# Second tile of q and k: loaded in fp32 by the hardware DMA queues and cast on chip

## The chip, the cores and the metric

The kernel runs on one core of one Trainium2 chip. The metric is device time in microseconds for one execution, the median over several runs of the same program. A profiled execution is shown beside it, with its own span.

## The reference

Attention with a sliding window of 128 tokens and four "sink" tokens that every token sees, then a layer norm and a two-layer MLP with a residual. Batch 4, 8 heads, 768 tokens, head size 64, so the MLP works on rows of 512 with an inner size of 2048. All inputs and the output are fp32.

```python
scores = (1/sqrt(D)) * q @ k.T
keep   = (pos_k < n_sink) | ((0 <= pos_q - pos_k) & (pos_q - pos_k < window))
a      = softmax(where(keep, scores, -1e9))
x      = (a @ v) with the heads side by side            # (B, S, 512)
xn     = (x - mean(x)) / sqrt(var(x) + 1e-6) * g_ln
out    = x + relu(xn @ w_ch1) @ w_ch2
```

## The kernel before

**Tiling.** The 3072 tokens are 24 tiles of 128 (`t`), two to a chunk (`c`, twelve chunks, three to a batch element). Per chunk: load q and k, bring them into the transposed layout `kq` (head size on the partitions), multiply for the scores (`sc`), exponentiate on ScalarE (`ex`), mask on VectorE (`mk`), multiply with v (`av`), divide by the row sum (`rc`, `x`), take mean and variance (`bn`, `ag`), center (`xc`), transpose (`trx`, copied out by `evx`), and then the MLP: `ph` is the first layer, in eight blocks per chunk, `rl` its relu on ScalarE, `pc` or `p1` to `p7` the second layer. The first two chunks are handled tile by tile, the rest by chunk.

**Order.** Every step is an operation of a planner (`Plan`) with a priority, the engines that may run it and a cost. `Plan.run` simulates all queues and gives each engine a fixed order; the program is then written out in that order. So a changed cost or a changed set of operations can change the order on any engine. Waits between engines come from semaphores. PE is also given filler matmuls on a `junk` tile where the plan has it idle in the first 24 us.

**Queues.** Three DMA queues matter. SP and ACT issue plain copies (the hardware queues). GpSimd (POOL) issues the copies that cast from fp32 to bf16 (the casting queue); nearly all inputs come that way. The program has eight completion semaphores for the hardware queues together and eight for the casting queue; a ninth transfer of a kind waits at its issue until the first has landed.

**The first chunk.** This is what the change touches. Tile 0 of q and k comes in fp32 by SP and ACT, four transfers of 128 KB (`kld00*`, `qld00*`, line 620) into the buffer `n4a`. It is cast to bf16 on chip in two halves (`cast0` on ScalarE, `cast1` on VectorE, line 637), transposed on PE (`tr000`, `tr001`, line 649) and copied from PSUM into `kq` in four pieces (`ev00**`, line 595, 128x256 each). Tile 1 comes by the casting queue, already bf16, into two `nat` buffers (`kld01`, `qld01`, line 626). It needs no cast: PE transposes it (`tr010`, `tr011`, line 645) and VectorE copies it out in two pieces of 128x512 (`ev010`, `ev011`).

**The order of the first loads on POOL**: `kld01`, `qld01`, `vld0` (v of tile 0), `kld1`, `qld1` (k and q of chunk 1, 256 KB each as bf16, into `n4b`, line 602), `vld1`, `w1ld0`, `w1ld1` (the first two quarters of the first MLP weight, 512 KB each, line 547), `vld2`, `w1ld2`, `vld3`, `w1ld3`, `kld2`, `qld2` (chunk 2, into `n4c`), and so on.

**The order on PE around it**: `tr000 tr001 sc0_0 tr010 tr011 sc1_0 gtt av0 pm11 sc1_1 tr10 tr11 trx0 av1 vp0 sc2_0 sk1 sc2_1 sc3_0 ph0_0 trx1 sc3_1 ph0_1 sv2 av2 ph0_2 sv3 ph0_3 ph0_4 trx2 av3 ph0_5 ph1_0 ph0_6 trx3 ph0_7 ph1_1 tr20 tr21 ...`; **on ScalarE**: `cast0 ev0000 ev0010 ex0_0 ex1_0 ex1_1 ev11 ex2_0 sx1 ex2_1 ex3_0 ex3_1 rl0_0 rl0_1 ...`; **on VectorE**: `cast1 ev0001 ev0011 kts0 ev010 ev011 gt rc0 x0 bn0 ag0 xc0 ev10 evx0 rc1 x1 bn1 ag1 xc1 mk2_0 evx1 mk2_1 vs0 mk3_0 mk3_1 rc2 ...`. Here `tr10`, `tr11` transpose chunk 1, `gtt` and `gt` bring in the layer norm's weight (a load of 2 KB on SP, line 526), `vp0` and `vs0` prepare the sink values, `sk` and `sx` are the sink scores and their exponential, `sv` the sink values' product, `kts0` packs the sink keys.

Of the kernel before, what the change touches and what calls it, by code (L numbers as in the profile page):

```python
# [236 lines left out]
NEG = -1e30  # L237
NEVER = -1e9

PAR = dict(split=(3, 4, 5, 6, 7), gsum=-8.0, guard=183.0, strict=40.0, win=0.4, tr=-8.0, sc=-5.3, sc1=-2.0, av=2.0, trx=9.0, by_dma=4, x_by_dma=2, g_on_w=2, av2=20.0, avi=1.0, behind=5, gtt=9.0, ramp=0.3, vs0=2.6, vpb=12.0,  # L240
           w1p=(0.15, 1.7, 2.05, 2.8), pm=2, w2p=(4.5, 4.51, 4.52, 4.53), by_tile=2, wino=2, vp=(0.0, 0.1, 2.0, 2.1, 4.2, 4.3), ld1=0.05,
           h=dict(av=1.62, avi=0.4, sc=-7.53, sc1=-3.14, tr=-20.67, trx=9.0, xo=-11.34), mkp=(0,), mko=-3.48, vsp=1, soon=0, lb=0, xlag=2.1, llag=2.4, mix=(1.0, 0.5), tzp=16.19, kp=-0.9, half=4, wsum=58.0, flip=1, te=("POOL",), tlead=33.28, rd=0, cpr=20.34, sp=(10.74, 5.73), sq=(-5.24, -23.14, 6.14, 23.93), pos=(0.11, 1.67, 2.3, 8.33, 1.63, 2.3, 3.91), pos4=(7.29, 3.8, 1.67, 7.72))

# [130 lines left out]
def kernel(  # L374
# [218 lines left out]
    def evict(name, prio, n, src, dst, reads, writes, fp=False):  # L593
        du = {"ACT": act(n), "DVE": dve(n) if fp else dve(n, 0.52)}
        P.op(name, du, prio, lambda e: (nc.scalar.copy if e == "ACT" else V.tensor_copy)(dst(), src()),  # L595
             reads=reads, writes=writes)

    def load4(c, nm, prio, loaded):
        b, R = c // RC, c % RC
        p0 = 64 * "kq".index(nm)  # L600
        ap = (k if nm == "k" else q)[b, :, 256 * R:256 * R + 256, :].rearrange("h (p i) d -> p h (i d)", i=4)
        P.op(f"{nm}ld{c}", {"POOL": (0.72, 0.75)}, prio, lambda e: G.dma_start(
            n4_b[c].t[p0:p0 + 64].rearrange("p h i d -> p h (i d)"), ap), writes=[loaded, n4_b[c]], dma=SW_4)

    def chunk(c):
# [3 lines left out]
        T = Buf(f"kq{c}", "kq")  # L609
        kq_b[c] = T  # L610
        if c == 0:
            f0, c0 = n4_b[0], Buf("c0", "hq")
            raw = lambda: f0.t.rearrange("p h i d -> p (h i d)").bitcast(FP32).rearrange("p (h i d) -> p h i d", h=4, i=4)
            cut = lambda: c0.t.rearrange("p a b -> p (a b)")[:, 0:1024].rearrange("p (i h d) -> p i h d", i=4, h=4)
            for x, src in enumerate((k, q)):
                for hh in range(2):
                    ap = src[b, 4 * hh:4 * hh + 4, 0:128, :].rearrange("h (p i) d -> p h (i d)", i=4)
                    p0 = 64 * x + 32 * hh
                    P.op(f"{'kq'[x]}ld00{hh}", {("SP", "ACT")[x]: (0.53, 0.53)}, -110 + hh, lambda e, p0=p0, ap=ap:
                         (nc.sync if e == "SP" else nc.scalar).dma_start(  # L620
                             raw()[p0:p0 + 32].rearrange("p h i d -> p h (i d)"), ap), writes=[f0], dma=HW_F)
            nat = []
            for x, (nm, src) in enumerate((("k", k), ("q", q))):
                nat.append(Buf(f"{nm}n01", "nat"))
                ap = src[b, :, 128:256, :].rearrange("h p d -> p h d")
                P.op(f"{nm}ld01", {"POOL": (0.87, 0.9)}, -50 + 0.1 * x, lambda e, nat=nat[x], ap=ap: G.dma_start(nat.t, ap),  # L626
                     writes=[nat[x]], dma=(SW[0] + PAR["ramp"] * (1 - x), *SW[1:]))
            for t in range(2):
                for hh in range(2):
                    hs = slice(4 * hh, 4 * hh + 4)  # L630
                    pt, half = Buf(f"pt0{t}{hh}", "one"), Buf(f"c0{hh}")
                    done = Buf(f"T0{t}{hh}") if t or not hh else tile_of[0, 0]
                    tile_of[t, hh] = done
                    if t == 0:
                        two = slice(2 * hh, 2 * hh + 2)
                        P.op(f"cast{hh}", {"DVE": dve(512), "ACT": act(512)}, early(0) + 0.01 * hh, lambda e, two=two:
                             (nc.scalar.copy if e == "ACT" else V.tensor_copy)(cut()[:, :, two], raw()[:, two].rearrange("p h i d -> p i h d")),
                             reads=[f0], writes=[c0, half])

                    def tr(e, pt=pt, t=t, hh=hh):  # L640
                        pb = pt.t.bitcast(BF16)[:, 0:512]
                        if t:
                            for h in range(2):
                                for x in range(2):
                                    nc.tensor.transpose(pb.rearrange("p (h k c) -> p h k c", h=2, k=2)[:, h, x],
                                                        nat[x].t[:, 4 * hh + 2 * h:4 * hh + 2 * h + 2, :], ident)
                        else:
                            for i in range(4):
                                nc.tensor.transpose(pb[:, 128 * i:128 * i + 128], cut()[:, i, 2 * hh:2 * hh + 2], ident)
                    P.op(f"tr0{t}{hh}", pe(0.3), early(t) + 0.02 + 0.1 * hh, tr, reads=[*(nat if t else [half]), Bc["ident"]],  # L650
                         hold=[T] + ([] if t else [c0]), writes=[pt])
                    if t:
                        evict(f"ev0{t}{hh}", early(t) + 0.05 + 0.1 * hh, 512,
                              lambda pt=pt: pt.t.bitcast(BF16)[:, 0:512].rearrange("p (m c) -> p m c", m=4),
                              lambda hs=hs: T.t[:, hs.start // 2:hs.start // 2 + 2, :, 128:256].rearrange("p h k c -> p (h k) c"), [pt], [T, done])
                    for a in () if t else range(2):
                        evict(f"ev00{hh}{a}", early(0) + 0.05 + 0.1 * hh + 0.01 * a, 256,
                              lambda pt=pt, a=a: pt.t.bitcast(BF16)[:, 0:512].rearrange("p (i k a g) -> p a k g i", i=4, k=2, a=2)[:, a],
                              lambda a=a, hh=hh: T.t[:, 2 * a + hh, :, 0:128].rearrange("p k (g i) -> p k g i", i=4), [pt], [T, done], fp=True)
        elif c < PAR["by_dma"]:  # L660
            loaded = Buf(f"l{c}")
            for i in range(2):
# [250 lines left out]
    def weight_sums():  # L913
        a = [w1[m][:, 2 * i:2 * i + 2, :] for m in range(2) for i in range(2)]
        get = {n: (lambda i=i: a[i]) for i, n in enumerate(("a11", "a12", "a21", "a22"))}
        held = [Buf(f"ws{i}", "hq") for i in range(2)]
        for i, (x0, x1, op) in enumerate((("a21", "a22", ALU.add), (0, "a11", ALU.subtract),
                                          ("a11", "a21", ALU.subtract), ("a12", 1, ALU.subtract))):
            done = Buf(f"wsum{i}")
            ap = lambda i=i: held[i // 2].t[:, 2 * (i % 2):2 * (i % 2) + 2, :]  # L920
            val = lambda x: ap(x) if isinstance(x, int) else get[x]()
            P.op(f"wsum{i}", {"DVE": dve(1024, 0.52)}, PAR["wsum"] + 3.0 * i, lambda e, ap=ap, x0=x0, x1=x1, op=op, val=val:
                 V.tensor_tensor(ap(), val(x0), val(x1), op=op), reads=Bw1g[0:2] + [wsum[x][1] for x in (x0, x1) if isinstance(x, int)],
                 hold=[held[i // 2]], writes=[done], nb=PAR["wsum"] + 3.0 * i)
            wsum.append((ap, done, held[i // 2]))

# [145 lines left out]
                     reads=[ot, oo], dma=HW_S)  # L1072

    def wino(c, T, hq, h1, quick):
        A = [lambda g=g: hq[g].t.rearrange("p (v k) (s t) -> p k v s t", k=2, s=2) for g in range(2)]
        part = {"a11": lambda g: A[g]()[:, 0, :, :, 0:128], "a21": lambda g: A[g]()[:, 0, :, :, 128:256],
                "a12": lambda g: A[g]()[:, 1, :, :, 0:128], "a22": lambda g: A[g]()[:, 1, :, :, 128:256]}
        if quick:
            h1 = [None] * 4 + h1
        deps = {n: [quick[int(n[1]) - 1] if quick and g == 0 else h1[4 * g + (0 if n[2] == "1" else 1)::2][:2] for g in range(2)] for n in part}  # L1080
        sb = {}

        def get(n, g):
# [80 lines left out]
    for c in range(NC):  # L1164
# [5 lines left out]
            attend_tile(2 * c + 1)  # L1170
        else:
            attend(c)
    idle = [[o for z in n4_b if z.ring == f"n4{x}" for o in z.users] for x in "bca"] + [[]]
    for qt in range(4):
        b11, b12, b21, b22 = (w2[qt][:, 2 * i:2 * i + 2, 256 * j:256 * j + 256] for i in range(2) for j in range(2))
        t1, t2, t3, t4 = (w2t[i][:, qt] for i in range(4))
        for i, (o, x0, x1) in enumerate(((t1, b12, b11), (t2, b22, t1), (t3, b22, b12), (t4, b21, t2))):
            P.op(f"w2t{i}_{qt}", {"DVE": dve(512, 0.52)}, 16.0 * PAR["wino"] - 6.0 + qt + 0.1 * i, lambda e, o=o, x0=x0, x1=x1: V.tensor_tensor(
                o, x0, x1, op=ALU.subtract), reads=[Bw2[qt]] + ([Bw2t[i - 1][qt]] if i in (1,) else [Bw2t[1][qt]] if i == 3 else []),
                writes=[Bw2t[i][qt]], after=idle[i])  # L1180

# [98 lines left out]
```

## Time and profile before

| | |
|---|---|
| median of 3 runs | 208.51 us (208.4 to 208.91) |
| profiled execution, its own time | 208.16 us |
| its span | 206.6 us, TensorE at the full granted clock (1.0) |
| PE busy | 199.4 us, 97% of the span |
| DVE, ACT, POOL busy | 179.6, 119.7, 118.7 us |
| casting queue | 13.37 MB written as bf16, 81.7% of the 16 DMA engines' span |
| hardware queue of SP | 13.43 MB, 34.1% |

The profiled execution took 208.16 us, of which its span is 206.6. The remaining 1.6 us lie around the program. A row of the timeline gives the start, the duration, the engine, the line, the operation and how many instructions it merges, and in brackets how long the engine sat idle before it and what ended that. GB/s counts the bytes written; a casting transfer reads twice what it writes.

### The profile page before, as it was taken

To read this page: it belongs to the slowest core of one execution; us is meant where nothing else is said; L and a number is where in the kernel's file an instruction comes from. 1 tells how busy PE (TensorE), PEld (TensorE's weight loads), DVE (VectorE), ACT (ScalarE), POOL (GpSimd) and SP (SyncE) were. 2 spreads that over 40 slices of the span, in tenths; PEclk is the share of its full clock that TensorE was granted. 3 is DMA by queue.
4 is the path that set the end of the run, shared out by engine and by line. 5 is a ranking of instruction groups with operands and counts; after the bars stand their busy time and mean duration, and the time that the engine had idled before them with its cause. 6 is when DMAs were issued, how large, how long until landed. Compare 5 with 4: busy or idle time off the path is not lost.

```text
span 206.6 us, 6790 instructions
## 1 busy us (share of the span) xinstructions
PE 199.4 (97%) x2766; PEld 165.6 (80%) x2766; DVE 179.6 (87%) x437; ACT 119.7 (58%) x187; POOL 118.7 (57%) x170
## 2 busy tenths in 40 slices
PE   6888999999999999999999999999999999999994
PEld 2557996674698897898998988988988988988993
DVE  7589769899599899899989989989989989998693
ACT  3649477839555655666486486485486585560620
POOL 7977475279039029959649949968627229125000
PEclk9999999999999999999999999999999999999999
DMA  5999999999999999999999999899976411210302
GB/s 117 146 195 195 197 181 205 199 158 171 186 200 124 124 191 101 121 174 101 175 152 137 113 159 143 109 171 114 194 117 101 128 33 23 106 32 19 108 27 84
DMA packets 101341, 27.55 MB, mean 133 GB/s; under 512 B 89652, under 2 KB 99128, under 8 KB 101304
## 3 DMA queue, kind: packets, MB, share of 16 engines
q0 software_dynamic: 67712, 13.37, 81.7%
q1 hardware_dynamic: 33304, 13.43, 34.1%
q8 instruction: 22, 0.36, 0.7%
q10 hardware_dynamic: 288, 0.26, 0.4%
q14 instruction: 15, 0.12, 0.2%
HBM read 27.31 MB, written 6.29 MB: 163 GB/s over the span
## 4 chain that ended last, share of the span: by engine, by line
PE 90%; DMA 3%; DVE 3%; POOL 2%; issue 0%; DVEq 0%
PE one L1109 31%; PE one L1027 20%; PE one L958 12%; PE one L1058 7%; PE one L1020 7%; PE pair L854 5%; PE pair L802 4%; DMA n4b<-in_q_dram 3%; PE one L672 1%; PE pair L721 1%; POOL nat L626 1%; PE one L714 1%; DVE xnt L907 1%; DVE kq L595 1%; POOL vn L589 0%; DVE st L874 0%
## 5 line engine op out<-in xcount | busy, mean ns | idle before, releaser
L1027 PE MATMUL one<-xnt,w 128*128 128x256 bf16 x384 | 46.8, 273 | 0.0
L814 ACT ACTIVATE pe<-pair 128x1024 bf16<-128x1024 f32 (+1 forms) x40 | 36.3, 963 | 18.2 <-PE pair L802 18.2
L1037 ACT ACTIVATE hq<-one 128x512 bf16<-128x512 f32 x58 | 33.4, 590 | 17.9 <-PE one L1020 9.4
L1027 PEld LDWEIGHTS <-w 128*128 128x128 bf16 x384 | 36.3, 98 | 4.0
L1109 PEld LDWEIGHTS <-hs 128*128 128x128 bf16 x320 | 31.0, 98 | 4.0
L882 POOL TENSOR_SCALAR st<-st 128x1 f32<-128x1 f32 x24 | 6.4, 266 | 44.4 <-DVE rec L868 27.5
L826 DVE TENSOR_TENSOR pe<-pe,mask 128x1024 bf16<-128x1024 bf16 (+1 forms) x35 | 27.1, 799 | 1.6 <-ACT pe L814 1.4
L969 ACT COPY tz<-one 128x512 f32<-128x512 f32 x24 | 13.9, 585 | 20.6 <-PE one L958 19.2
L1109 PEld LDWEIGHTS <-hq 128*128 128x128 bf16 x240 | 22.2, 98 | 4.1 <-issue 0.5
L589 POOL DMA_DIRECT2D vn<-in_v_dram x24 | 21.9, 922 | 2.2 <-DMA w<-in_moe_w_ch_dram 1.2
L983 ACT ACTIVATE hq<-hq 128x512 bf16<-128x512 bf16 x24 | 15.1, 630 | 13.1 <-DVE hq L980 12.6
L1109 PE MATMUL one<-w,hq 128*128 128x256 bf16 x160 | 19.2, 273 | 0.0
L980 DVE TENSOR_TENSOR hq<-one,tz 128x512 bf16<-128x512 f32 x24 | 16.4, 684 | 1.9 <-PE one L958 1.0
L1130 DVE TENSOR_TENSOR ot<-one,tm 128x256 f32<-128x256 f32 x40 | 15.9, 412 | 2.1 <-PE one L1109 1.8
L1123 DVE TENSOR_TENSOR tm<-one,x 128x256 f32<-128x256 f32 x40 | 16.6, 414 | 1.2 <-PE one L1109 1.1
L870 DVE TENSOR_TENSOR x<-pair,rec 128x512 bf16<-128x512 f32 x24 | 16.6, 691 | 0.8
L874 DVE BATCH_NORM_STATS2 st<-x 128x6 f32<-128x512 bf16 x24 | 16.5, 687 | 0.2
L1020 PE MATMUL one<-xnt,w 128*128 128x128 bf16 x256 | 16.0, 219 | 0.5 <-DVE xnt L907 0.5
L687 POOL DMA_DIRECT2D nat<-in_q_dram x16 | 14.2, 893 | 3.7 <-DMA w<-in_moe_w_ch_dram 3.7
L938 POOL TENSOR_TENSOR xt<-xnt 128x256 bf16<-128x256 bf16 x16 | 12.2, 778 | 7.1 <-DMA xnt<-xc 7.0
L687 POOL DMA_DIRECT2D nat<-in_k_dram x16 | 14.8, 928 | 2.4 <-DMA w<-in_moe_w_ch_dram 2.4
L1020 PEld LDWEIGHTS <-w 128*128 128x128 bf16 x256 | 14.6, 98 | 1.6 <-issue 0.8
(130 smaller groups left out, 387.7 us busy)
## 6 DMA issues: line engine op xcount, KB each, us to landing
out_dram<-ot SPq DMA_DIRECT2D x17, 256.0 KB
w<-in_moe_w_ch_dram POOLq DMA_DIRECT2D x8, 512.0 KB, 12.8
vn<-in_v_dram POOLq DMA_DIRECT2D x24, 128.0 KB, 6.9
nat<-in_k_dram POOLq DMA_DIRECT2D x17, 128.0 KB, 4.6
nat<-in_q_dram POOLq DMA_DIRECT2D x17, 128.0 KB, 4.9
out_dram<-ot SPq DMA_DIRECT2D x14, 128.0 KB
kq<-nat SPq DMA_TRANSPOSE x32
xnt<-xc SPq DMA_TRANSPOSE x20
```

What stands on the lines that cost most here:

```text
L589: loads[b * RB + r, "v"] = P.op(f"vld{t}", {"POOL": (0.87, 0.9)}, prio, lambda e: G.dma_start(bv.t[:, :, 0:64], v[b, :, 128 * r:128 * (r + ...
L687: lambda e, nat=nat, ap=ap: G.dma_start(nat.t, ap), writes=[nat], dma=SW if c < 6 else (*SW[:2], PAR["llag"]), after=behind(c, 0 if soon e ...
L814: P.op(f"ex{c}{hp}", {"ACT": act(2 * n)}, d + 0.1 + 0.05 * j, lambda e, pp=pp, pb=pb: nc.scalar.activation(pb.t[:, :, 0:n], pp.t[:, :, 0:n ...
L826: V.tensor_mul(pb.t[:, :, 0:n], pb.t[:, :, 0:n], mm),
L870: P.op(f"x{t}", {"DVE": dve(512)}, d + xo + 0.11, lambda e: V.tensor_tensor(x.t.rearrange("p (a h c) -> p a h c", a=2, c=64), pv()[:, :, : ...
L874: P.op(f"bn{t}", {"DVE": fix(0.60)}, d + xo + 0.12, lambda e: V.bn_stats(st.t[:, 8:14], x.t), reads=[x], writes=[st, mv])
L958: nc.tensor.matmul(b.t[:, 128 * h:128 * h + 128], lhsT=lt[:, kk, 128 * h:128 * h + 128], rhs=rh[:, kk, :], start=first and h == 0 and kk = ...
L1020: nc.tensor.matmul(ph.t[:, 128 * s:128 * s + 128], lhsT=w1[u // 2][:, j, 128 * s:128 * s + 128], rhs=xnt.t[:, j, 128 * (u % 2):128 * (u % ...
L1027: nc.tensor.matmul(ph.t[:, 256 * s:256 * s + 256], lhsT=w1[ht // 4][:, j, 128 * (ht % 4):128 * (ht % 4 + 1)], rhs=xnt.t[:, j, :], start=j ...
L1037: nc.scalar.activation(hg.t[:, u % 4, :], ph.t, AF.Relu)
L1109: nc.tensor.matmul(at(r), lhsT=get(left, g)[:, v, s, :], rhs=rhs, start=first and n == 0, stop=n == 7, skip_group_check=True)
L1123: return P.op(f"tm{name}_{c}", {"DVE": dve(256, 1.14)}, pr - PAR["kp"], lambda e: V.tensor_tensor(tm[name].t, at(r), xs[i].t[:, sl], op=AL ...
```

## The change

Tile 1 of q and k is handled as tile 0 is. Four more transfers of 128 KB are issued on SP and ACT right behind those of tile 0, into the buffer `n4c` (which later takes chunk 2, and is free until then). Two casts (`cast10`, `cast11`), two groups of four transposes and four 128x256 copies (`ev01**`) take the place of the two casting loads, eight transposes and two 128x512 copies. The planner's cost of such a hardware load is 0.42 instead of 0.5. Other edits in the diff only name constants (`w2tp`, `we`, `c1p`) at the values that were there, or rewrite `wino` for a case that doesn't occur.

```diff
-HW_F = (0.5, 0.9, 0.9)
+HW_F = (0.42, 0.9, 0.9)
...
         if c == 0:
-            f0, c0 = n4_b[0], Buf("c0", "hq")
+            for t in range(2):
+                f0, c0 = (n4_b[0], Buf("r0b", "n4c"))[t], Buf(f"c0{t}", "hq")
+                n4x.append(f0)
...
+                for x, src in enumerate((k, q)):
+                    for hh in range(2):
+                        ap = src[b, 4 * hh:4 * hh + 4, 128 * t:128 * t + 128, :].rearrange("h (p i) d -> p h (i d)", i=4)
+                        p0 = 64 * x + 32 * hh
+                        P.op(f"{'kq'[x]}ld0{t}{hh}", {("SP", "ACT")[x]: (0.53, 0.53)}, -110 + 2 * t + hh, ...
+                             (nc.sync if e == "SP" else nc.scalar).dma_start(
+                                 raw()[p0:p0 + 32].rearrange("p h i d -> p h (i d)"), ap), writes=[f0], dma=HW_F)
...
-            for x, (nm, src) in enumerate((("k", k), ("q", q))):
-                nat.append(Buf(f"{nm}n01", "nat"))
-                ap = src[b, :, 128:256, :].rearrange("h p d -> p h d")
-                P.op(f"{nm}ld01", {"POOL": (0.87, 0.9)}, -50 + 0.1 * x, lambda e, nat=nat[x], ap=ap: G.dma_start(nat.t, ap),
-                     writes=[nat[x]], dma=(SW[0] + PAR["ramp"] * (1 - x), *SW[1:]))
...
+                    P.op(f"cast{t}{hh}", {"DVE": dve(512), "ACT": act(512)}, early(t) + 0.01 * hh + (PAR["c1p"] if t else 0.0), ...
+                         (nc.scalar.copy if e == "ACT" else V.tensor_copy)(cut()[:, :, two], raw()[:, two].rearrange("p h i d -> p i h d")),
+                         reads=[f0], writes=[c0, half])
...
-                    if t:
-                        evict(f"ev0{t}{hh}", early(t) + 0.05 + 0.1 * hh, 512,
...
+                    for a in range(2):
+                        evict(f"ev0{t}{hh}{a}", early(t) + 0.05 + 0.1 * hh + 0.01 * a, 256,
```

The planner's new orders, up to where they meet the old ones again. **POOL**: `kld1 vld0 qld1 vld1 w1ld0 w1ld1 vld2 w1ld2 vld3 w1ld3 kld2 qld2 ...` and from there as before. **PE**: `tr000 tr001 sc0_0 tr010 gtt av0 tr011 sc1_0 tr10 pm11 sc1_1 trx0 tr11 sc2_0 vp0 av1 ph0_0 sc2_1 sk1 sc3_0 trx1 sc3_1 ph0_2 ph0_1 sv2 av2 sv3 ph0_3 av3 ph0_4 trx2 ph0_5 ph0_6 ph0_7 trx3 ph1_0 tr20 tr21 ph1_1 ...`; from the end of chunk 1's MLP on (`ph2_0`) the order on PE is that of before. **ScalarE**: four issues, `tab`, then `cast00 cast01 ev0000 ev0010 ex0_0 cast11 ev0100 ev0101 ev0110 ev0111 ex1_0 ev10 ex1_1 ex2_0 rl0_0 ex2_1 sx1 ex3_0 ex3_1 rl0_2 rl0_1 ...`. **VectorE**: `ev0001 ev0011 kts0 cast10 gt rc0 x0 bn0 ag0 xc0 evx0 ev11 rc1 x1 bn1 ag1 xc1 mk2_0 evx1 mk2_1 vs0 mk3_0 mk3_1 rc2 ...`.

More of the change, by code (lines that the diff above doesn't have):

```diff
@@ L656, in chunk @@
-                    for a in () if t else range(2):
-                        evict(f"ev00{hh}{a}", early(0) + 0.05 + 0.1 * hh + 0.01 * a, 256,
+                    two = slice(2 * hh, 2 * hh + 2)
+                    P.op(f"cast{t}{hh}", {"DVE": dve(512), "ACT": act(512)}, early(t) + 0.01 * hh + (PAR["c1p"] if t else 0.0), lambda e, two=two, raw=raw, cut=cut:
+                         (nc.scalar.copy if e == "ACT" else V.tensor_copy)(cut()[:, :, two], raw()[:, two].rearrange("p h i d -> p i h d")),
+                         reads=[f0], writes=[c0, half])
```

63 lines of the change are left out of this document (22 added, 41 removed).

## The prediction

> **What bounds the kernel now.** I read the page first.
>
> ```profile
> span 206.6 us, 6790 instructions
> PE   6888999999999999999999999999999999999994
> ```
>
> After the first four slices (20 us) PE has no slack left. From the end of chunk 1 on PE's order is the same in both kernels, so what the change is worth is how much earlier, or later, PE reaches the work that fills it: a shift of the start. The profiled execution took 208.16 us, 0.35 less than the median of 208.51; the sum is made against 208.16 and carried over to the median. About 0.3% (0.63 us) is what a measurement of this kernel can tell from no change.
>
> Second, the chain that ended last, at its beginning.
>
> ```profile
> 1.99 1.08 POOL nat L626
> 3.07 0.90 POOL nat L626
> 3.98 0.88 POOL vn L589
> ...
> 5.50 7.09 DMA n4b<-in_q_dram
> 12.73 0.65 PE one L672 x16
> 13.41 1.23 DVE kq L595
> ...
> 18.75 1.05 PE one L1020 x16
> 20.61 0.89 PE one L1020 x16
> ```
>
> The start hangs on the casting queue: two `nat` issues that the change removes, `vld0`, then `qld1`, whose landing at 12.59 lets PE transpose chunk 1. Last, the timeline of the same stretch.
>
> ```profile
> 1.02 0.90 ACTq L620 DMA_DIRECT2D n4a<-in_q_dram  x2
> ...
> 1.95 1.28 ACT L481 ACT_TABLE_LOAD   x1 [1.95 <-PEq L1261]
> ...
> 5.04 0.62 ACT L637 CAST hq<-n4a 128x512 bf16<-128x512 f32 x1 [1.59 <-DMA n4a<-in_q_dram]
> ...
> 6.43 0.65 ACT L595 COPY kq<-one 128x256 bf16<-128x256 bf16 x2 [0.78 <-PE one L649]
> ...
> 7.05 1.55 POOL L547 DMA_DIRECT2D w<-in_moe_w_ch_dram  x2
> ...
> 7.63 0.41 DVE L695 COPY kts<-kq 64x16 bf16<-64x16 bf16 x2
> ...
> 7.82 0.62 PE L645 MATMUL one<-ident,nat 128*128 128x128 bf16 x8
> 7.92 1.02 ACT L758 ACTIVATE pe<-pair 128x1024 bf16<-128x1024 f32 x1 [0.84 <-PE pair L754]
> ...
> 9.16 1.02 ACT L758 ACTIVATE pe<-pair 128x1024 bf16<-128x1024 f32 x1 [0.22 <-PE pair L754]
> ...
> 10.19 0.42 PE L854 MATMUL pair<-vn,pe 128*128 128x65 bf16 x8 [0.91 <-ACT pe L758]
> ...
> 13.85 1.01 ACT L595 COPY kq<-one 128x1024 bf16<-128x1024 bf16 x1 [0.66 <-PE one L672]
> ...
> 13.98 0.65 PE L854 MATMUL pair<-vn,pe 128*128 128x65 bf16 x16
> ...
> 15.15 0.20 DVE L868 RECIPROCAL rec<-pair 128x8 f32<-128x8 f32 x1
> ...
> 16.15 0.27 ACT L769 ACTIVATE ps<-one 128x128 bf16<-128x128 f32 x1
> ...
> 16.56 2.85 ACT L758 ACTIVATE pe<-pair 128x1024 bf16<-128x1024 f32 x3
> ...
> 19.29 1.15 ACT L1037 ACTIVATE hq<-one 128x512 bf16<-128x512 f32 x2
> ...
> 19.55 1.28 DVE L761 TENSOR_TENSOR pe<-pe,mask 128x1024 bf16<-128x1024 bf16 x2
> ...
> 19.74 0.28 PE L721 MATMUL pair<-vs,ps 32*128 32x260 bf16 x2
> ...
> 24.16 2.84 PE L1020 MATMUL one<-xnt,w 128*128 128x128 bf16 x48
> ```
>
> Two things are to be seen. Tile 1's first exponential (`ex1_0`, 9.16) runs before `av0` (10.19). And `av0` is put down to ScalarE, but its exponential had ended at 8.94: what came at 10.19 was v of tile 0, as the landing below shows. `av0` waits for `vld0`.
>
> **The DMA side.** The next rows are stretches of one microsecond (last column GB/s written) and single transfers (last column: us from issue to landing).
>
> ```profile
> 2.00:3.00 1.00, 1.00 (x3) 0.30 (x2) 1.00 (x9) 1.00 (x1) 1.00 (x1) 1.00 0.67 179
> 3.00:4.00 1.00, 1.00 (x4) 0.35 (x3) 0.87 (x6) 0.44 (x2) 1.00 (x3) 1.00 1.02 335
> 4.00:5.00 1.00, 1.00 (x5) 0.45 (x4) 0.96 (x6) 0.00 (x0) 1.00 (x2) 1.00 0.90 67
> 6.00:7.00 1.00, 1.00 (x15) 0.66 (x11) 0.16 (x1) 0.56 (x2) 1.00 (x2) 1.00 1.98 129
> 9.00:10.00 1.00, 0.28 (x6) 0.23 (x2) 0.17 (x2) 0.83 (x1) 1.00 (x2) 1.00 1.37 174
> ```
>
> ```profile
> vn<-in_v_dram POOLq DMA_DIRECT2D x1, 128.0 KB, 6.2
> n4b<-in_q_dram POOLq DMA_DIRECT2D x1, 256.0 KB, 7.1
> w<-in_moe_w_ch_dram POOLq DMA_DIRECT2D x1, 512.0 KB, 8.8
> w<-in_moe_w_ch_dram POOLq DMA_DIRECT2D x1, 512.0 KB, 10.8
> ```
>
> Tile 0's four transfers are 524 kB and are what moved from 2 to 4 us (179 + 335 kB); ScalarE could cast at 5.04, about 1.0 after the last bytes. Then follows a gap: 67 kB in the microsecond from 4 to 5, half of what the casting queue moves once it runs (129).
>
> *Removed*: 2 x 131 kB from the casting queue, at 129 kB a us 2.0 us; and 1.08 + 0.90 us of issue on POOL. *Added*: 524 kB on the hardware queues, at 335 kB a us 1.6 us, of which about 0.5 fall into the gap. So all that stands behind on the casting queue comes 2.0 - 1.6 + 0.5 = 0.9 us earlier, by this estimate: `qld1` at 11.7 instead of 12.59, `w1ld0` at about 15.0 (before: issued at 7.05, 8.8 to landing, 15.85), `w1ld1` at 17.7 (before: issued at 7.8, landed at 18.6). The ends: 0, if the two kinds of transfer hinder each other by as much as is saved, and 2.0, if the added ones cost the casting queue nothing.
>
> [...]
>
> *`vld0` itself* is less sure. It is issued about 1.0 earlier (second in the queue instead of third; 256 KB of `kld1` ahead of it in place of the two `nat`), which by its 6.2 us gives 9.1. But the 1.6 us of hardware traffic now stand in its way, less 0.5 of gap and 2.0 - 1.5 for `kld1` at 174 instead of `nat` at 129: 0.6 later, 10.8. I take 9.8, between the two: by 10.19 the queue had moved far more than `vld0` and what stood ahead of it, so bytes alone don't set its landing.
>
> *Covered at no cost*: the two more issues on ACT (0.45 each) push the table load to 2.9, done by 4.4 with its first use, before 5.04; if the cover went, tile 0's cast would wait, and that would still be 1.2 us short of `av0`. On SP eight hardware loads use all eight semaphores, so the load of the layer norm's weight and the `vc` loads wait for tile 0's landing at 5.0 rather than being issued from 1.93 on; `gtt` needs the weight at 9.06 and the `vc` loads are first needed in chunk 3. The second fp32 set lands between 6.6 (alone) and 8.1 (sharing half the engines): 4.0 + 1.6 or 3.1, + 1.0. VectorE takes `cast10` after `kts0`, at 8.04, ScalarE `cast11` after `ex0_0`, at 8.94. Both casts of tile 0 are now on ScalarE (0.62 each, to 6.28 instead of 5.79 on two engines), but its copies out of PSUM alternate between the engines as before, and tile 0 stays at 7.6. Were it later, `ex0_0` and `cast11` follow one to one.
>
> **The chain of tile 1.** On PE the order is now `tr010 gtt av0 tr011 sc1_0`: the second half of tile 1 is queued behind `av0`, which waits for `vld0`. Behind them stand `sc1_0` and everything of chunk 1. With `vld0` at 9.8, `av0` ends at 10.25, `tr011` (four of the eight transposes in 0.62) at 10.55. ScalarE has all four 128x256 copies (0.33 each): `ev0110` ends at about 11.0, the other half of `sc1_0` waits for it, and `ex1_0` starts at 11.35, 2.2 us later than the 9.16 of before. If `vld0` came at once, `cast11` would set it: 9.55 + 1.1 = 10.7.
>
> From there ScalarE is the chain: `ex1_0` to 12.4, `ev10` (1.01) 13.4, `ex1_1` 14.4, `ex2_0` 15.4. `av1` runs from 14.45 to 15.1 (before: 13.98). `ph0_0` follows at 15.15, since `w1ld0` is there; `rl0_0` (0.6) ends at 16.75, `ex2_1` at 17.8, `sx1` and two exponentials of 0.95 at 20.0; before, the last of these ended at 19.41. VectorE's row from `rc1` to `evx1` is the same list as before: there it began at 15.15 and let PE go at 18.75; now it begins at 15.2. Then `mk2_1`, `vs0` and the two masks, which ended at 20.83, 2.1 us behind `evx1`, end near 20.9, or 1.28 after the exponentials, 21.2 at the latest.
>
> So tile 1 is about half a us later. What pays for it is the order on PE: `ph0_0` and, from 18.3, `ph0_2` run where PE stood idle, with weights that came 0.9 earlier. Counted on: `ph0_2` to 19.2, `ph0_1` 20.1 (0.89 each), `sv2`, `av2`, `sv3` 21.2 (0.28 and 0.65 a piece), `ph0_3` 22.1, `av3` 22.75, `ph0_4` 23.65, `trx2` about 23.9. Before, PE had the same set behind it at 24.16, where the group of 48 matmuls begins. The sum is 24.16 - 23.9 = 0.25 us gained: 207.9 on the profile's scale, 208.3 as a median. Each us by which `vld0` lands otherwise moves the result by as much, in both directions, break-even being a landing at about 10.05; earlier than 9.1 gains nothing more, as `cast11` and `w1ld0` then set the pace.
>
> **The rivals.**
>
> *The queue is relieved in full.* `vld0` lands by 9.2 and the weights come 1.5 to 2 us earlier: `ex1_0` at 10.7, and the set is done 0.65 earlier still, a gain of 0.9: 207.6. For it: `nat` was the slowest traffic in the rows (129 against 174), and the issue is a us earlier. Against: the hardware traffic stands in exactly this stretch.
>
> *`vld0` is held up by the hardware traffic.* It lands at 10.8 or 11.0 instead of 10.19, and, unlike before, half of tile 1's transposes wait behind `av0`: `ex1_0` at 12.4, ScalarE's row ends past 21, the set at 24.9 to 25.1: 0.75 to 0.95 slower, 209.3 to 209.5. It decides as soon as `vld0` lands after 10.7. For it: PE's new order and the bytes ahead. Against: the issue is earlier. [...]
>
> *The change buys nothing of what it says.* The second fp32 set lands after 9, so that `cast10` is what `tr010`, and with it `av0` and `tr011`, wait for; each us past 8.9 costs one. At 9.9 it is 209. Against: 1.6 us of traffic that starts at 4.0.
>
> **How the numbers follow.** Within 0.3% of 208.51 (the forecast, `vld0` between 9.4 and 10.7): 0.40. Faster by more: 0.31. Slower by more: 0.24 for the held-up `vld0` and 0.05 for the late casts, 0.29 together. The likeliest case alone spans 207.9 to 209.1. The range reaches to the sums of both main rivals, 207.5 to 209.4, and leaves out what lies beyond them, about 2 in 10.
>
> **What would show it.** Right: `ex1_0` near 11.4 and waiting on PE; `av0` near 9.8 with the landing of `vn` as its release; `kld1` and `qld1` landing near 11.7; `w1ld0` near 15.0; the first `L1020` group (line 1004 then) at 15.2; the same row of 48 or fewer matmuls after `trx2` near 23.9; from 30 us on every PE group shifted by one constant, about -0.25. Wrong: a shift that grows along the run, a drop of the granted clock from 1.00 in the thinner stretch from 11 to 18 us, a wait of PE for a weight after 20 us, or `vld0` landing outside 9.1 to 10.8.

## The result and the profile after

| | median us | runs | lowest to highest |
|---|---|---|---|
| before | 208.94 | 22 | 208.25 to 210.04 |
| after | 211.12 | 22 | 208.76 to 213.02 |

The ratio is 1.0067, 95% interval 1.0042 to 1.0091: slower, about 209.9 on the scale of 208.51. The prediction was 208.3 (207.5 to 209.4). The ratio leaves out the executions that lie over 1.5% above a kernel's fastest; the medians alone give 1.0104, and why the changed kernel has so many long executions is part of what follows.

The page of the changed kernel's profile (an execution of 211.73 us): of PE's busy share in 40 slices the third digit (10.5 to 15.8 us) is now 7, where it was 8.

```profile
span 210.0 us, 6794 instructions
...
PE   6979999999999999999999999999999999999993
```

Its timeline. Columns: start, duration, engine and line, operation and tiles; in brackets the idle time before it and what ended it. (Lines are shifted: 632 casts, 638 transposes, 742 exponentials, 838 `av`, 877 `trx`, 1004 `ph`.)

```profile
3.78 0.71 POOL L604 DMA_DIRECT2D n4b<-in_q_dram  x1
...
5.22 1.14 ACT L632 CAST hq<-n4a 128x512 bf16<-128x512 f32 x2 [0.79 <-DMA vc<-in_v_dram]
...
8.85 1.02 ACT L742 ACTIVATE pe<-pair 128x1024 bf16<-128x1024 f32 x1 [0.79 <-PE pair L738]
9.21 0.43 DVE L632 CAST hq<-n4c 128x512 bf16<-128x512 f32 x1 [0.30 <-DMA n4c<-in_q_dram]
9.77 0.61 ACT L632 CAST hq<-n4c 128x512 bf16<-128x512 f32 x1
11.48 0.42 PE L838 MATMUL pair<-vn,pe 128*128 128x65 bf16 x8 [1.00 <-DMA vn<-in_v_dram]
11.73 0.39 PE L638 MATMUL one<-ident,hq 128*128 128x128 bf16 x4
12.90 1.02 ACT L742 ACTIVATE pe<-pair 128x1024 bf16<-128x1024 f32 x1
16.29 1.06 PE L1004 MATMUL one<-xnt,w 128*128 128x128 bf16 x16
24.75 0.39 PE L877 MATMUL one<-ident,xc 128*128 128x128 bf16 x4
```

Four things are late. Tile 0's first exponential starts at 8.85 (7.92 before). The second fp32 set lands at 9.2. v of tile 0 is there at 11.48 (before 10.19), and PE stands idle until then with half of tile 1 queued behind `av0`. Tile 1's first exponential starts at 12.90 (9.16). The first block of the MLP is nevertheless 0.4 us earlier (16.29 against 16.68).

The transfers (last column: us from issue to landing). q of chunk 1, issued at 3.78, lands at 12.7; before it was 12.6. So the casting queue is no earlier for what stands behind.

```profile
n4b<-in_k_dram POOLq DMA_DIRECT2D x1, 256.0 KB, 7.5
...
n4b<-in_q_dram POOLq DMA_DIRECT2D x1, 256.0 KB, 8.9
```

The view that shows why is the DMA view cut to single microseconds: packets, MB and busy share of each queue. `q0` is the casting queue, `q1` and `q10` are the hardware queues. After, from 4 to 5 and from 5 to 6 us:

```profile
q10 hardware_dynamic: 137, 0.13, 47.4%
q1 hardware_dynamic: 140, 0.13, 47.1%
q0 software_dynamic: 5, 0.00, 1.8%
...
q0 software_dynamic: 103, 0.05, 39.0%
q1 hardware_dynamic: 89, 0.08, 33.4%
q10 hardware_dynamic: 50, 0.04, 26.6%
```

Before, from 5 to 6 us:

```profile
q0 software_dynamic: 1082, 0.14, 214.4%
q1 hardware_dynamic: 18, 0.00, 1.9%
```

While the hardware queues have the second fp32 set to move, the casting queue moves 0.00 and 0.05 MB a microsecond; alone it moved 0.14. The first transfers in the queue differ between these two kernels, though. Two of the runs below differ in the hardware traffic alone (the removal alone, then both halves of the traffic). There the casting queue moves 0.07 MB without the traffic and nothing with it from 4 to 5 us, and from 5 to 6 us:

```profile
q0 software_dynamic: 598, 0.12, 159.9%
```

```profile
q0 software_dynamic: 213, 0.03, 42.3%
```

How much of the start is lost is best read from one row that has the same form in both kernels, the score products (line 802 before, 786 after). Before, then after:

```profile
82.21 0.25 PE L802 MATMUL pair<-kq,kq 64*64 64x64 bf16 x4
```

```profile
83.43 0.25 PE L786 MATMUL pair<-kq,kq 64*64 64x64 bf16 x4
```

The shift is +1.22 us, and it is +1.22 on all such rows from 64 to 83 us (ahead of that the two orders on PE still differ). Below, "shift" is always this row's start less 82.21. Behind it the profiled execution loses another 2.35 us (211.73 - 208.16 - 1.22). The profile of before is of a short execution (208.16, where the median of the series is 208.94): against it every other profile here, the second one of before too, loses 0.7 us or more behind 83 us. In the changed kernel 1.04 us of this loss show as waits on PE, two for VectorE (0.57 together) and one for a transfer:

```profile
125.39 0.33 PE L786 MATMUL pair<-kq 64*64 64x192 bf16 x8 [0.47 <-DMA kq<-nat]
```

### The profile page after: what moved, and what is told of

Its sections match the earlier page's. It is cut to its first block, busy times and chain, and to the rows that moved or that the text cites. A ratio compares the mean times of both kernels' runs of the same rounds, so it can differ in the third digit from the quotient of the medians.

```text
span 210.0 us, 6794 instructions
## 1 busy us (share of the span) xinstructions
PE 201.5 (96%) x2757; PEld 166.1 (79%) x2762; DVE 180.4 (86%) x434; ACT 121.8 (58%) x194; POOL 116.8 (56%) x168
## 5 line engine op out<-in xcount | busy, mean ns | idle before, releaser
L1021 ACT ACTIVATE hq<-one 128x512 bf16<-128x512 f32 x59 | 34.1, 590 | 19.6 <-PE one L1004 11.0
L967 ACT ACTIVATE hq<-hq 128x512 bf16<-128x512 bf16 x24 | 15.1, 630 | 13.9 <-DVE hq L964 13.4
L1096 PE MATMUL one<-w,hq 128*128 128x256 bf16 x160 | 19.2, 273 | 0.0
L922 POOL TENSOR_TENSOR xt<-xnt 128x256 bf16<-128x256 bf16 x16 | 12.5, 796 | 6.0 <-DMA xnt<-xc 6.0
```

What stands on the lines that cost most here:

```text
L1021: nc.scalar.activation(hg.t[:, u % 4, :], ph.t, AF.Relu)
L1096: nc.tensor.matmul(at(r), lhsT=get(left, g)[:, v, s, :], rhs=rhs, start=first and n == 0, stop=n == 7, skip_group_check=True)
```

## Experiments

The theories. A: the hardware traffic holds up the casting queue, v of tile 0 above all, and tile 1 is queued behind it on PE. B: the second fp32 set itself is late. C: the thin stretch makes the granted clock drop in part of the executions. The last four runs are single executions on another chip of the same kind, where one execution of the kernel before took 210.78 us beside them; they are read for their traces.

**The changed kernel again.**

> The changed kernel once more, unaltered. If the loss is all in the start (late v of tile 0, late casts), its executions should lie close together, some 0.6 to 1.2 us above the kernel before (the start was 1.2 us late in the first profile). If a drop of TensorE's granted clock is a second cause, they should fall into two groups again: near 209.2 with a clock of 0.998 to 1.0, near 211.5 with 0.991 to 0.997.

Measured: ratio 1.0046 (0.9996 to 1.0095), median 211.11, from 208.07 to 213.88. The profile fell on an execution of 213.12, and serves here for its mechanism alone: v was there at 12.29, the second fp32 set at 9.8, and the row by stretches shows the clock (third column from the end: granted clock; the first pair: the stretch's length and PE's busy time):

```profile
10.00:12.00 2.00, 0.59 (x5) 0.46 (x6) 0.43 (x2) 1.07 (x3) 0.82 (x1) 1.00 2.51 133
12.00:14.00 2.00, 1.53 (x28) 1.18 (x30) 1.11 (x3) 0.92 (x3) 0.86 (x3) 0.89 1.57 184
14.00:16.00 2.00, 2.00 (x24) 0.92 (x20) 1.02 (x3) 1.74 (x2) 1.84 (x4) 0.50 1.24 203
16.00:18.00 2.00, 2.00 (x37) 1.46 (x34) 1.16 (x2) 1.23 (x2) 1.27 (x2) 0.76 1.51 198
```

In steps of half a microsecond the clock is 0.50 from about 13.6 to 16.9, after PE had been busy for 0.59 of 2 us. The shift is +2.67. One such stretch of 3.4 us at half takes the mean clock of 210 us to 0.992. Over both series of this kernel 14 of 32 executions have a mean clock of 0.992 or less, median 211.9; the other 18 have 209.9. Where the drop lies in the executions without a profile is not shown. Of 55 executions of the kernel before measured beside them none is below 0.997.

**`av0` behind tile 1** (a change of order only; traffic as after; `put(a, b, d)` gives `a` the place just behind `b`, or ahead of it where d is negative).

```
+ put("av0", "sc1_0", 1e-5), put("rc0", "sc1_0", 2e-5), put("x0", "sc1_0", 3e-5)
```

> The changed kernel with one move in PE's order: av0 (with rc0 and x0 on VectorE) stands behind tr011 and sc1_0, as in the kernel before, instead of ahead of them. Theory A (v of tile 0 is held up by the hardware traffic, and tile 1 queues behind it): tr011 no longer waits for v, ex1_0 starts near 11.7 instead of 12.90 (then the cast that ends at 10.38 sets it), and the start is 0.8 to 1.2 us earlier: median about 1 us lower than the changed kernel. Theory B (the second fp32 set itself is late, landing at 9.2): little is gained, ex1_0 at 11.7 but the end within 0.4 us. Theory C (the clock): the share of executions with a clock under 0.998 stays.

Measured: 1.0073 (1.0032 to 1.0115). Theory A's gain is missed; two of ten executions have a mean clock of 0.992 or less (five of ten in the repeat). The profile (an execution of 209.55, shift +0.68) is no test of the wait for v, as v landed at 10.0 in it, within what the prediction had allowed. One wait on PE for the casting queue shows in it:

```profile
12.22 0.50 PE L656 MATMUL one<-ident,n4b 128*64 128x128 bf16 x11 [0.70 <-DMA n4b<-in_q_dram]
```

Chunk 1's q ends that wait 0.5 us earlier than in the kernel before (12.73), and still the start is late. The edit itself holds `av0` back to 11.08, and with it the work on VectorE that chunk 1's second transposes stand behind. So the run does not say where the time goes.

**v of tile 0 first in the casting queue** (the same transfers, `vld0` issued ahead of `kld1`).

```
+ put("vld0", "kld1", -1e-5)
```

> The changed kernel with v of tile 0 issued first on the casting queue, ahead of k of chunk 1, and nothing else moved. Theory A: it lands by 9.5 to 10.3 instead of 11.48, av0 runs right behind gtt at about 10.5, ex1_0 near 11.9 and the median is about 0.8 us lower. Theory B: av0 gains as much, but ex1_0 stays above 11.7 and the median within 0.4 us. If the hardware traffic holds up whatever is first on the casting queue, v lands no earlier than 11.

Measured: 1.0035 (0.9997 to 1.0072), median 209.5; ten executions, none with a clock below 0.997. From its timeline and its transfers:

```profile
9.63 0.43 PE L838 MATMUL pair<-vn,pe 128*128 128x65 bf16 x8
...
11.07 1.02 ACT L742 ACTIVATE pe<-pair 128x1024 bf16<-128x1024 f32 x1
```

```profile
n4b<-in_q_dram POOLq DMA_DIRECT2D x1, 256.0 KB, 6.9
```

v (issued at 2.15) lands at 8.2, `av0` no longer waits for it, q of chunk 1 (issued at 3.98) lands at 10.9, and the shift in this execution (208.59) is -0.52. In the DMA view the hardware queues are nearly done by 6 us here (0.02 MB left from 6 to 7), and from 6 to 7 the casting queue moves 0.15 MB (0.10 in the changed kernel, beside 0.10 of hardware traffic). That so small a change of order goes with earlier landings of both kinds was not foreseen, and why stays open. The intervals of this ratio and of the change's own overlap, so the gain in time is likely (median 209.5 against 211.1) and not proven.

**The hardware traffic alone** (the kernel before, with the four fp32 loads of tile 1 added; nothing reads them).

```
+ o.emit = lambda e: (was(e), (nc.sync if e == "SP" else nc.scalar).dma_start(spare[p0:p0 + 32], ap))
```

> The kernel before with only the hardware transfers added: tile 1 of q and k is also loaded in fp32 into the spare buffer and never used; the casting loads stay. Theory A: 524 kB more beside the casting queue delay nat q (7.47 before) to about 8.5 to 9, v of tile 0 (10.16) to about 11.5, all behind it by 1.0 to 1.6 us, and the time rises by 0.8 to 1.5 us. If the gap from 4 to 5 us hides most of the added traffic, v lands by 10.6 and the time rises by less than 0.5 us.

Measured: 1.0127 (1.0032 to 1.0223; four executions). Its timeline and transfers:

```profile
8.87 0.56 PE L645 MATMUL one<-ident,nat 128*128 128x128 bf16 x7 [0.49 <-DMA nat<-in_q_dram]
...
10.57 0.42 PE L854 MATMUL pair<-vn,pe 128*128 128x65 bf16 x8 [0.30 <-DMA vn<-in_v_dram]
```

```profile
n4b<-in_q_dram POOLq DMA_DIRECT2D x1, 256.0 KB, 8.5
```

q of chunk 1, issued at 5.50, lands at 14.0, 1.4 us later than before; the shift is +1.14. That is theory A's first half by itself, with no cast and no change of order. It holds for q of chunk 1. v, which theory A names first, is there at 10.57, not at the 11.5 that it expected: 0.4 later than in the first profile of before, whose own v came 0.9 later than in the second (10.2 and 9.3).

**PE kept busy with filler** (seven junk multiplications of 512 columns between `gtt` and `av0`).

```
+ if o.name == "av0":
+     items += [(o.start - 1e-4, -512, ones[...]) for _ in range(7)]
```

> The changed kernel with seven more junk multiplications of 512 columns (0.21 us each, 1.5 us) on PE between gtt and av0, where PE stood idle from 10.1 to 11.5 us (10.4 to 12.3 in the repeat, after which the granted clock was 0.50 from 13.6 to 16.9 us). Nothing else is moved. Theory C (the idle stretch while av0 waits for v lets the granted clock drop in part of the executions, at a price of about 1.5 to 2 us each): no execution, or one in ten, shows a mean clock below 0.996, and the median falls from 211.1 to 209.3 to 209.8, ratio 1.003 to 1.005. Theory A alone (only the late landing of v and the work queued behind av0): the start shift stays +1.2 us and the median stays near 211. Against both: the junk itself delays av0, and the time rises by up to 0.3.

Measured: 1.0080 (1.0054 to 1.0107), median 210.71, from 209.74 to 211.38. Half of theory C's expectation is met: none of ten executions is below 0.997, and the upper tail (up to 213.9) is gone. The other half is not: the median did not fall to 209.8. The filler costs the good executions (lowest 209.74 instead of 208.07). In the profile the second fp32 set lands at 10.2, v at 11.5, and `av0` begins only behind the filler, 1.2 us after v; the expectation had allowed 0.3 for that. The shift is +1.69. From the timeline:

```profile
10.22 0.43 DVE L632 CAST hq<-n4c 128x512 bf16<-128x512 f32 x1 [1.44 <-DMA n4c<-in_q_dram]
...
11.18 1.47 PE L1225 MATMUL one<-junk 128*128 128x512 bf16 x6
...
12.70 0.42 PE L838 MATMUL pair<-vn,pe 128*128 128x65 bf16 x8
```

So with PE kept busy the drops are gone (0 of 10 against 14 of 32); what they cost can't be read from this run, because the filler is itself in the way.

**The removal alone.**

```
+ ops[x + "ld01"].emit = lambda e: None          # x in "kq": no casting loads of tile 1
+ ops["tab"].emit = ...                          # ScalarE writes zeros in their place
```

> The kernel before without tile 1's two casting loads (tile 1's q and k are zeros written by ScalarE, so that part of the computation is left out). It prices the removal alone. Prediction's term: 2.0 us of casting traffic gone and 1.98 us of issue on POOL, so v of tile 0 lands near 8.2 (10.2 before), q of chunk 1 near 10.6 (12.59), the first expert weight near 13.9 (15.85); the start is then 1.0 to 1.5 us earlier and the median 207.3 to 207.8. Theory A (bytes of the shared engines decide): the same. Rival (a casting transfer's landing is set by its own count of pieces and not by what stands ahead): the landings move by less than 1 us and the time by less than 0.3 us.

Measured: 0.9950 (0.9917 to 0.9982), median 208.13 beside 208.91: 1.0 us by the ratio. q of chunk 1, issued at 3.98, lands at 10.0, 2.6 us earlier than before, and v, first in the queue here, at 6.3 (10.2 before); the shift is -1.24. The expectation had 2.0 us for either, so the rival, that landings hardly move, is out.

**Both halves of the traffic, none of the casts.**

> The kernel before with both halves of the traffic change, none of the work that hangs on it: tile 1's casting loads are gone (zeros as in the run without them) and the fp32 hardware loads of tile 1 are there, unused. What is left out is tile 1's real q and k. v of tile 0 is first in the casting queue here. If the two effects add (about +1.4 us from the hardware traffic, -1.5 to -2 from the removal), q of chunk 1 lands between 11.5 and 12.5, and the time is within 0.5 us of before. With v first, theory A expects a landing of v before 9.5 and no wait of av0 over 0.5 us; theory C expects a clock of 0.996 or more in nearly all executions. If the median is at 209.5 as in the kernel with v first, the casts and copies of tile 1 cost nothing; if it is at 208.5 or below, they cost the difference.

Measured: 1.0017 (0.9984 to 1.0050), median 209.29; clock 0.997 or more in all ten. The transfers of v and of chunk 1's q in the removal alone, then in both halves:

```profile
vn<-in_v_dram POOLq DMA_DIRECT2D x1, 128.0 KB, 4.1
n4b<-in_q_dram POOLq DMA_DIRECT2D x1, 256.0 KB, 6.0
```

```profile
vn<-in_v_dram POOLq DMA_DIRECT2D x1, 128.0 KB, 6.6
n4b<-in_q_dram POOLq DMA_DIRECT2D x1, 256.0 KB, 7.6
```

The added hardware traffic takes back 1.6 of the 2.6 us on q of chunk 1, which lands at 11.6, and 2.5 us on v, which lands at 8.7. By the ratios it takes back 0.0067, or 1.4 us, about what the removal brings (1.0): the net, 1.0017, can't be told from none, and the shift of the profile is -0.17. Tile 1's casts and copies, which the kernel with v first has on top, cost 0.0018 by the ratios, which can't be told from none either.

**v first, and work given back to VectorE.**

```
+ ops["vld0"].start = ops["kld1"].start - 1e-5
+ for name in ("cast01", "ev0101", "ev0111"):
+     ops[name].eng = "DVE"
```

> The changed kernel with v of tile 0 first in the casting queue, one cast of tile 0 given to VectorE (as before the change) and two of tile 1's four copies out of PSUM given to VectorE. Theory A: v lands near 9.3 as in the kernel with v first, tile 0's transposes start 0.4 us earlier, tile 1's first exponential at about 10.3 (11.2 with v first alone, 12.9 in the changed kernel), start shift -0.7 to -1.0 against before; median 208.0 to 209.0. Theory C: clock 0.996 or more in nearly all. Rival: what v first left over (209.5 against 208.7) does not come from the start but from a later stretch; then the median stays at 209.3 or more although the profile shows the start ahead.

Measured: 1.0052 (1.0011 to 1.0092), median 210.05, and the ten times fall apart: three of 208.4 to 208.7, five of 210.4 to 211.2. The expectation of 208.0 to 209.0 is missed. The profiled execution (208.42) had a shift of -0.47. Two more profiles were taken to see a late one.

> A second profile of the kernel with v first, one cast and two copies on VectorE, whose ten times lay between 208.4 and 211.2 and whose one profile was of a 208.4 execution. Theory A (landings vary from execution to execution): where the execution takes over 210, the second fp32 set lands after 9.0 (8.1 or before in the first profile) and the shift is there by 32 us. Rival (a later stretch): the start is the same, -0.5 at 64 us, and the loss comes behind 100 us.

> A third profile of the same kernel, with the same question: a slow execution with a late start (landing of the second fp32 set after 9.0), or with the same start and a loss behind 100 us.

The cast of the second fp32 set on VectorE in the three profiles, of executions of 208.42, 209.95 and 210.44 us:

```profile
8.16 0.80 DVE L632 CAST hq<-n4c 128x512 bf16<-128x512 f32 x1
```

```profile
8.68 0.43 DVE L632 CAST hq<-n4c 128x512 bf16<-128x512 f32 x1 [0.56 <-DMA n4c<-in_q_dram]
```

```profile
9.27 0.43 DVE L632 CAST hq<-n4c 128x512 bf16<-128x512 f32 x1 [1.04 <-DMA n4c<-in_q_dram]
```

q of chunk 1 landed at 10.6, 11.8 and 12.4, and the shifts are -0.47, +0.29 and +1.57. The landings of one program differ by more than a microsecond between these executions, and the time goes with them. The first of the three ran on the other chip, but on that chip, too, three kernels with the same transfers (the change repeated, `av0` behind tile 1, filler) had v at 12.3, 10.0 and 11.5. In the last of the three the clock dropped as well, to 0.50 from 12.7 to 16.1, though no gap on PE was over 0.9 us and PE had been busy for about 2.1 of the 3.4 us before:

```profile
12.00:14.00 2.00, 1.50 (x18) 0.84 (x18) 1.32 (x4) 1.24 (x2) 1.07 (x3) 0.67 1.25 204
14.00:16.00 2.00, 2.00 (x25) 1.29 (x26) 0.50 (x1) 1.49 (x2) 1.75 (x4) 0.50 1.32 199
```

The second profile has a loss behind 83 us too (its shift grows from 0.29 to 1.42 at 109 us), so the rival, a later stretch, holds a part.

**The hardware transfers alone.** GpSimd reads the second fp32 set before its first issue, so the casting queue stands still until it has landed.

```
+ G.tensor_copy(rec[:, NT - 1, 0:1], second[:, 0:1])     # ahead of kld1's issue
```

> The changed kernel with the casting queue held back: GpSimd reads one column of the second fp32 set ahead of its first issue, so no casting transfer runs beside the hardware transfers. It measures the hardware transfers alone. If the second fp32 set is late in the changed kernel (9.2 to 10.2 us in three profiles) because it shares the engines with the casting queue, it lands between 5.6 and 6.6 here: 524 kB at the 335 kB a us of the first set is 1.6 us after 4.0, and about 1 to the landing. If it is late by itself (its issues at 2 to 3 us, its pieces), it lands after 8. From there the casting queue runs alone: v of tile 0 takes 6.2 us or less from its issue, q of chunk 1 7.1 or less. The time is about 2 to 3 us above the kernel before, as the queue starts 3 us later.

Measured: 214.07 us, 4.7 us above the kernel before on that chip in the next run and 3.3 above the other execution there; the expectation was 2 to 3. The shift is +4.95. The read that ends when the set has landed, two stretches of the DMA traffic (last column GB/s), and two of PE's long wait for v:

```profile
7.16 0.18 POOL L1203 COPY rec<-n4c 128x1 f32<-128x1 f32 x1 [5.17 <-DMA vc<-in_v_dram]
```

```profile
5.00:6.00 1.00, 1.00 (x5) 0.41 (x4) 0.00 (x0) 0.87 (x2) 0.00 (x0) 1.00 0.82 264
6.00:7.00 1.00, 1.00 (x13) 0.65 (x11) 0.05 (x1) 0.73 (x3) 0.00 (x0) 1.00 0.10 31
...
12.00:13.00 1.00, 0.00 (x0) 0.00 (x0) 0.00 (x0) 0.00 (x0) 1.00 (x3) 0.71 2.13 159
13.00:14.00 1.00, 0.00 (x0) 0.00 (x0) 0.00 (x0) 0.00 (x0) 1.00 (x2) 0.50 1.40 166
```

The second set has all but moved by 6 us and lands at 7.1, between what sharing (6.6 at most) and lateness of its own (after 8) had led one to expect: from 4 to 6 us it moved 228 and 264 kB a microsecond, not 335. So it is late by about half a microsecond on its own, in this one execution. Beside the casting queue it took until 9.2, 9.8 and 10.2 in three profiles with `kld1` first (8.7 or before in a fourth), and until 9.3 at the latest with v first. v takes 5.2 us from its issue and q of chunk 1 5.9, within the 6.2 and 7.1 expected of a queue that runs alone. And it is theory C's cleanest case: PE stood idle from 9.7 to 14.1, and the clock was 0.50 from 12.5 to 19.2.

**The kernel before again.**

> A second profile of the kernel before, unaltered, for the scatter of its start: the profile shown is of one of its faster executions (208.16; median 208.5 to 208.9). If the start of the kernel before scatters as little as its times, q of tile 1 lands between 7.6 and 8.1, v of tile 0 between 10.0 and 10.5, q of chunk 1 between 12.3 and 12.9, and the score products at 32, 64 and 108 us lie within 0.4 us of the first profile.

Measured: 209.41 us. Tile 1's transposes and the same score row:

```profile
5.76 1.38 PE L1236 MATMUL one<-junk 128*128 128x512 bf16 x5
6.93 1.01 PE L649 MATMUL one<-ident,hq 128*128 128x128 bf16 x8
...
9.03 0.62 PE L645 MATMUL one<-ident,nat 128*128 128x128 bf16 x8
...
82.41 0.25 PE L802 MATMUL pair<-kq,kq 64*64 64x64 bf16 x4
```

The expectation of steady landings is missed: q of tile 1 came at 7.1 and v at 9.3, both earlier than expected, and chunk 1's q at 12.7, as expected. Tile 1's transposes are late all the same (9.03 instead of 7.82), and no landing is the reason: PE ran slower for longer at the start (five filler matmuls in 1.38 us, 0.76 in the first profile; eight transposes of tile 0 in 1.01, 0.61 there), and tile 1 stands behind that work. The shift is met, +0.20. The kernel before has over a microsecond to spare in tile 1, because chunk 1's q, at 12.7, sets the start anyway. This execution also loses 1.0 us behind 82 us. So such losses are no property of the change, though at 2.3 us they are largest in the two profiles of the changed kernel; the run with both halves of the traffic, whose order is that of before, lost 2.1.

The steps side by side, by ratio: removal alone 0.9950, with the hardware traffic 1.0017, with the casts too (v first) 1.0035, with v behind `kld1` as in the change 1.0067. Neighbouring intervals overlap except between the first two, where they just fail to touch (0.9982 and 0.9984); the ends of the row are clearly apart. So it is shown that the added traffic eats what the removal brings; how the rest of the loss divides between the casts and the place of v is not. No version that computes tile 1 in full beat the kernel before.

## Why the prediction was wrong

**The chain from v's landing held.** The prediction said that each microsecond of `vld0` moves the result by as much, with break-even at 10.05. In the first profile v was there at 11.48, which gives +1.43; the measured shift was +1.22. `av0` was released by v, `tr011`, the copies and `ex1_0` followed as told (1.4 us from `av0` to `ex1_0`; 1.55 foretold), and the earlier MLP block did pay part of it back, though it came at 16.29, not at the 15.15 foretold.

**The term that failed is `vld0` itself**, taken at 9.8 between 9.1 and 10.8. It landed at 11.4 and 12.3 in the two profiles of this kernel, outside both ends; in two other kernels with the same transfers it came at 11.5 and, once, at 10.0. The part of it that was mis-sized is the charge for the hardware traffic, 1.6 - 0.5 = 1.1 us. With v first in the queue the traffic cost v 2.5 us (landing at 6.3 without it, 8.7 with it), and with `kld1` ahead of it v came another 2.7 later. The bounds counted bytes ahead of it at rates read from stretches in which one kind of queue ran alone.

**The stream term, 0.9 us earlier, came to about nothing.** Its parts were 2.0 for the removal (2.6 measured for q of chunk 1) and 1.1 for the added traffic (1.4 measured alone, 1.6 on top of the removal). Their sum holds, q at 11.6 against 11.7 foretold, but in the run that has v first, and because the two errors cancel, which is luck. With `kld1` first q landed at 12.7 (12.6 before), and at 12.1, 13.1 and 13.4 in three other profiles with that order. The first weight came at 15.6 (15.0 foretold, 15.8 before), the second at 18.8 (17.7 foretold, 18.6 before). The prediction did not ask whether the order within the casting queue changes what the hardware traffic costs it.

**The rates were those of either kind by itself.** The added traffic was charged at 335 kB a us, read on the hardware queues from 3 to 4 us, and the removal at 129, read on the casting queue from 6 to 7 us. Together, from 4 to 5 and from 5 to 6 us in the changed kernel, the two kinds moved 261 and 174 kB, of which the casting queue had 0.00 and 0.05 MB, and in the first of the two 5 packets against 277. Part of that is the casting queue's own start: held back until 7.7, it moved only 0.01 MB from 9 to 10 us. Part goes with the hardware traffic: from 5 to 6 us it moved 0.12 MB without that traffic and 0.03 with it. The DMA records agree: in the profile of before the casting queue's first packet started 2.1 us after its first issue began (1.94 to 4.00), in the changed kernel's 2.5 us after (1.95 to 4.42). What divides the time between the two kinds is not shown.

**The second fp32 set, 6.6 to 8.1, landed at 9.2.** Alone it landed at 7.1 in one execution; the 2 us on top are put down to the casting queue's traffic beside it, which the scatter of such landings (8.2 or before to 10.2) leaves uncertain. The rival of late casts was half right. In the profiled execution of the change v came last (the first half of tile 1 was transposed at 9.94, `av0` waited until 11.48). In the late execution with v first (the set at 9.27, v at 9.9) it was the cast that the transposes at 9.75, and behind them `av0`, waited for. Its price was slightly low: each microsecond past 8.9 on top of 208.3 gives 209.3 at 9.9, where it says 209.

**Tile 0 did not stay at 7.6.** Its first exponential came 0.9 late. Both casts on one engine account for about 0.5 (end at 6.36 instead of 5.8), slow transposes for the rest (1.03 us for eight, 0.61 before). The second profile of the kernel before has slow ones too (1.01), so that part is no property of the change: how long PE runs slowly at the start differs between executions.

**The clock was named as a sign and not priced.** A drop from 11 to 18 us stood in the list of what would prove the prediction wrong. By the mean clock it came in 14 of 32 executions, with a median 2.0 us above the others. Another sign on that list came true as well: the shift grew along the run, by 2.35 us behind 83 us. The second rival had the right mechanism and the right point of decision, 10.7; its 209.3 to 209.5 is short of 209.9 because its landing stopped at 11.0: at 11.48 its own rule gives 208.5 + 1.43 = 209.9. That the sum meets the ratio so closely is in part luck, as many of the executions with a drop of the clock are in the ratio too. The size of the drop is shown (0.50 for 3.4, 6.8 and 3.4 us in three profiles); how idle PE has to be for it is not: one execution (v first, with work given back to VectorE, 210.44 us) dropped after PE had been busy for about 2.1 of 3.4 us, and another (the hardware traffic alone, 210.68 us, mean clock 1.0) kept the full clock with PE busy for 1.85 us of the 3.4 from 12.54 to 15.96.

**What stays open**: why both queues finished earlier with v ahead of `kld1` (by 0.9 us for the second fp32 set and 1.4 for chunk 1's q on average of four profiles each, with ranges that overlap and two of the four from another chip), how the loss divides between that order and the casts, and the losses behind 83 us (0.7 to 2.3 us against the first profile of before), which all the kernels share, the one before among them.

## What to carry to other kernels

A transfer that leaves one queue for another can still hold up the queue it left: with the second fp32 set on the hardware queues the casting queue moved 0.03 MB from 5 to 6 us, 0.12 without it. So read the DMA view cut to single microseconds, with the bytes of each queue, at the place where the moved transfer will run, and ask who is moving there now. When a change moves a landing onto the critical path, its scatter from execution to execution comes with it (v of tile 0 at 10.0 to 12.3 with the same transfers); the old order had over a microsecond to spare in tile 1 (its transposes 1.2 us later in the second profile, the shift +0.20) and hid such lateness. Price the wait on PE twice: once as a wait, and once as the risk that the clock drops behind it (here to 0.50, for 3.4 to 6.8 us).

## What the runs showed of the hardware

- The granted clock was 1.00 or 0.50 in these rows (others are averages over a change). The three drops lasted 3.4 us (the change repeated), 6.8 (the casting queue held back) and 3.4 (v first, with work given back to VectorE, 210.44 us). In the clearest case, the second of these, PE stood idle from 9.7 and the clock fell at about 12.5.
- The landing of the same hardware transfers scattered between 8.2 or before and 9.3 us in four executions with v first (two on each of two chips), and between 8.7 or before and 10.2 in four with `kld1` first, though all were issued by 2.9 us.
- The casting queue started slowly even alone: issued at 7.72, it moved 0.01 MB from 9 to 10, 0.07 MB from 10 to 11 and 0.19 MB from 11 to 12. Its first packet started 2.1 us after the first issue in the profile of before, and 2.5 us after it beside the second fp32 set in the changed kernel's.
- Beside the second fp32 set, 524 kB on the hardware queues, the casting queue moved 0.03 MB from 5 to 6 us, 0.12 without it; its first transfer landed 2.5 us later (8.7 instead of 6.3).
